# FFT and routed mixture of experts on one core: the gate goes through the second block's gather as three integers, and one of its one-hot matrices gets a scheduling priority

## The chip, the cores and the metric

One core of a Trainium2 chip runs the whole program. Its engines work side by side, each through its own list of instructions in a fixed order: TensorE (PE, matmuls; its weight loads are shown as PEld), VectorE (DVE), ScalarE (ACT), GpSimd (POOL) and SyncE (SP, which here only issues DMAs). The metric is the device time of one execution in microseconds (us), lower is better.

## What is computed

The input x holds 8 batches of 2496 rows of 256 numbers. The real part of its two-dimensional Fourier transform, taken per batch, gives 19968 tokens of 256 numbers. Each token goes to the one expert of eight with the largest logit and is scaled by its softmax probability, the gate:

```python
X = np.fft.fft(np.fft.fft(x, axis=1), axis=2)
x = X.real.astype(np.float32).reshape(B * S, D)
logits = x @ w_gate + modality_bias[modality_id]
e_idx = np.argmax(logits, axis=1)
...
for e in range(E):                      # 8 experts, D = 256, F = 1024
    mask = e_idx == e
    h = np.maximum(x[mask] @ w1[e], 0.0)
    out[mask] = gate_w[mask, None] * (h @ w2[e])
```

## The kernel before

**Two streams of work.** One stream makes the transform and the route, batch by batch: an x tile is loaded (L388), folded on DVE (`fold_add`, the add of L399, 128x1280, and `fold`), its squares are summed on ACT (L402) and PE (L418) to get a scale, matmuls with constant matrices follow (L546; L570 to L590), ACT and DVE split the results into high and low half-precision parts (L524, L525, L221, L222; the tiles rp and rm hold the rows of tokens), and `route` finds the expert and the gate of each token on DVE (L646 to L673, one of them L663, which writes the one-hot choice oh), counts tokens before each other with a matmul by a triangle matrix (L703, L708, which read oh), and scatters the rows to a place per expert in memory (L801, POOL). The other stream prepares the weights of each expert: a load (L955, tile wa), sums of squares on ACT (L965, whose column goes to PE's L418), then a power-of-two scale and the split into a high half on ACT (L995) and a low half on DVE (L996), in tiles w_0, w_1 and w_2.

**Blocks.** Beside these, blocks of tokens run through an expert: L1211 is the first product (48 matmuls in a block of 128 tokens; per group of columns the third matmul reads the low half of the first half of w1, the sixth that of the second half), L1216 and L1217 write relu of it as high and low parts H, L1234 is the second product (24 matmuls, emitted one block later), L1238 and L1241 scale by the gate, L1242 scatters the result to the output. From about 210 us on the program is nearly only such blocks.

**The first three blocks** (128 tokens each, of experts 0, 1 and 2) do not read rows from memory. While the other rows of batch 0 are still on their way there, `onchip` gathers a block's tokens with matmuls: `onehot` (L766) writes a matrix of 117x1536 (12 groups of 128 columns) that has a one where a token's place in the expert's list is the column, PE multiplies rows by it (L782, 48 matmuls in 8 runs of six), ACT casts the result to xT (L785), and PE multiplies the same one-hot by pc (L788, 12 matmuls), a table of six half-precision columns per token: one, the low seven bits and the rest of the token's index, and the gate in three parts. DVE puts index and gate together again (L791 to L797, tile ig). `pieces` writes pc once for all three blocks. A half-precision gate part is the rounding of what the part before has left, times 2048, so L756 to L760 are a chain of five instructions. The one-hot lies in a buffer of its own name Pt, of which there is one, and the fold of x uses the same (L502 to L505).

**What sets the order.** The program is written as generators whose instructions a scheduler sorts, engine by engine, by priority and by its own estimate of times; `hp(n)` is a scope in which the instructions get n more priority. The order is fixed before the run. Two rules in the code tie instructions to `self.made`, the one-hot that was written last: the fold of batch 1 (L399) and the split of the second weight tile (w2 of expert 0) are issued after it.

Of the kernel before, what the change touches and what calls it, by code (L numbers as in the profile page):

```python
# [14 lines left out]
F32 = mybir.dt.float32  # L15
I32 = mybir.dt.int32
I16 = mybir.dt.int16
AF = mybir.ActivationFunctionType
ALU = mybir.AluOpType
# [3 lines left out]
P = 128  # L23
# [6 lines left out]
M3 = 117  # L30
# [219 lines left out]
class Kernel:  # L250
# [494 lines left out]
    def pieces(self, C, dst, gate, part, two):  # L745
        rt, V = self.rt, self.nc.vector
        pc = rt.tile([M3, C, 6], F16, name="pc", bufs=1)
        ix = rt.tile([M3, C], I32, name="pci", bufs=1)
        r = rt.tile([M3, C], F32, name="pcr", bufs=1)
        V.memset(pc[:, :, 0], 1.0)  # L750
        ids = two(self.ids[:, 0])
        V.tensor_scalar(part(ix), ids, 127, None, ALU.bitwise_and)
        V.tensor_copy(pc[:, :, 1], ix)
        V.tensor_scalar(part(ix), ids, 7, None, ALU.logical_shift_right)
        V.tensor_copy(pc[:, :, 2], ix)
        V.tensor_copy(pc[:, :, 3], gate)  # L756
        V.tensor_tensor(r, gate, pc[:, :, 3], ALU.subtract)
        V.tensor_scalar(pc[:, :, 4], r, 2048.0, None, ALU.mult)
        V.scalar_tensor_tensor(r, r, 2048.0, pc[:, :, 4], ALU.mult, ALU.subtract)
        V.tensor_scalar(pc[:, :, 5], r, 2048.0, None, ALU.mult)  # L760
        self.perm = C, dst, pc
        self.inv0 = self.inv[2]

    def onehot(self, C, dst, e):
        oh = self.oh = self.fft.tile([P, NH * P + P], F32, name="Pt", bufs=PQB).bitcast(F16)[:M3, 0:C * P].rearrange("p (c d) -> p c d", c=C)
# [3 lines left out]
    def onchip(self, e):  # L769

        nc, p, rt = self.nc, self.mo, self.rt
        V = nc.vector
        C, dst, pc = self.perm
        cols = [(r, j, s * group.ng + group.g0 + j) for s in range(2) for group in self.groups
                for r in (group.rows2[s],) for j in range(group.gn)]
        if e:
            self.onehot(C, dst, e)
        oh = self.oh
        ps = self.psf.tile([P, 512], F32, name="psf")
        for q in range(4):  # L780
            for k, (r, j, c) in enumerate(cols):
                nc.tensor.matmul(ps[:, q * P:(q + 1) * P], r.bitcast(F16)[:, j, q * P:(q + 1) * P], oh[:, c, :],  # L782
                                 start=k == 0, stop=k == C - 1)
        xT = p.tile([P, 4, P], I16, name="xT128", tag="xT", bufs=3).bitcast(F16)
        nc.scalar.copy(xT, ps.rearrange("p (q c) -> p q c", q=4))  # L785
        ps = self.psf.tile([P, 512], F32, name="psf")
        for k, (r, j, c) in enumerate(cols):
            nc.tensor.matmul(ps[:, 0:6], oh[:, c, :], pc[:, c, :], start=k == 0, stop=k == C - 1)  # L788
        ig = p.tile([P, 1, 2], F32, name="ig128", bufs=8)
        v = rt.tile([P, 6], F32, name="pcv", bufs=2)  # L790
        V.tensor_copy(v, ps[:, 0:6])  # L791
        V.scalar_tensor_tensor(v[:, 1:2], v[:, 2:3], 128.0, v[:, 1:2], ALU.mult, ALU.add)
        V.scalar_tensor_tensor(v[:, 1:2], v[:, 0:1], float(-OOB), v[:, 1:2], ALU.mult, ALU.add)
        V.tensor_scalar(ig.bitcast(I32)[:, 0, 0:1], v[:, 1:2], float(OOB), None, ALU.add)
        V.scalar_tensor_tensor(v[:, 4:5], v[:, 5:6], 1.0 / 2048, v[:, 4:5], ALU.mult, ALU.add)
        V.scalar_tensor_tensor(v[:, 3:4], v[:, 4:5], 1.0 / 2048, v[:, 3:4], ALU.mult, ALU.add)
        V.tensor_scalar(ig[:, 0, 1:2], v[:, 3:4], self.inv0, None, ALU.mult)  # L797
        return xT, ig

# [616 lines left out]
```

## Time and profile before

| | before |
|---|---|
| median of 3 runs | 1059.3 us (1054.3, 1059.3 and 1065.48) |
| the profiled execution, its own time | 1060.53 us |
| its span | 1058.1 us |
| mean granted clock of TensorE | 0.984 of full speed |
| PE busy / DVE busy | 1006.3 us / 560.3 us |

The span is what the trace covers; 2.4 us of the execution's own time lie around it. In a timeline a row is a run of like instructions: its start, its time, the engine, line, operation, output<-inputs, shape and count, and in brackets the idle time just before it with what ended that.

### The profile page before, as it was taken

To read this page: it belongs to the slowest core of one execution; us is meant where nothing else is said; L and a number is where in the kernel's file an instruction comes from. 1 tells how busy PE (TensorE), PEld (TensorE's weight loads), DVE (VectorE), ACT (ScalarE), POOL (GpSimd) and SP (SyncE) were. 2 spreads that over 40 slices of the span, in tenths; PEclk is the share of its full clock that TensorE was granted. 3 is DMA by queue.
4 is the path that set the end of the run, shared out by engine and by line. 5 is a ranking of instruction groups with operands and counts; after the bars stand their busy time and mean duration, and the time that the engine had idled before them with its cause. 6 is when DMAs were issued, how large, how long until landed. Compare 5 with 4: busy or idle time off the path is not lost.

```text
span 1058.1 us, 26309 instructions
## 1 busy us (share of the span) xinstructions
PE 1006.3 (95%) x10019; PEld 902.2 (85%) x10019; DVE 560.3 (53%) x1670; ACT 444.6 (42%) x886; POOL 371.0 (35%) x353
## 2 busy tenths in 40 slices
PE   6788999998999899999999999999999999999996
PEld 5585978986997799999899999988888888899995
DVE  4995969663876673675547553562222222222221
ACT  6674777443534433443334333332323232323331
POOL 0255264263245423443433333343554121221111
PEclk9998999998999999999999999999999999999999
DMA  9678896799499497746966583659888997597790
GB/s 351 248 264 289 200 327 274 195 307 288 132 272 324 138 313 182 210 145 179 285 188 184 163 257 101 192 184 272 214 257 252 301 260 192 149 281 177 205 205 26
DMA packets 151874, 237.66 MB, mean 225 GB/s; under 512 B 115804, under 2 KB 118757, under 8 KB 133565
## 3 DMA queue, kind: packets, MB, share of 16 engines
q1 hardware_dynamic: 132365, 193.75, 63.1%
q0 software_dynamic: 19376, 42.16, 12.4%
q8 instruction: 81, 1.33, 0.5%
q14 instruction: 52, 0.43, 0.1%
HBM read 206.37 MB, written 60.48 MB: 252 GB/s over the span
## 4 chain that ended last, share of the span: by engine, by line
PE 79%; ACT 5%; DVE 4%; issue 4%; DMA 4%; another core or an unknown queue 2%; POOL 1%; SPq 0%; POOLq 0%; ACTq 0%; DVEq 0%
PE pso L1234 35%; PE psm L1211 35%; DMA wa<-w 3%; PE psf L570 2%; PE psf L588 2%; PE psf L544 2%; ACT wj L965 2%; PE psf L575 1%; PE psf L590 1%; DVE H L1217 1%; ACT w L995 1%; ACT H L1216 1%; DMA XM<-x 1%; DVE w L996 1%
## 5 line engine op out<-in xcount | busy, mean ns | idle before, releaser
L1211 PE MATMUL psm<-xT,w 128*128 128x256 f16 (+1 forms) x4512 | 460.1, 258 | 10.2 <-issue 5.7
L1234 PE MATMUL pso<-w,H 128*128 128x256 f16 x3864 | 456.0, 273 | 6.4 <-issue 5.9
L1211 PEld LDWEIGHTS <-w 128*128 128x128 f16 x4512 | 386.9, 98 | 49.0 <-issue 11.4
L1234 PEld LDWEIGHTS <-H 128*128 128x128 f16 x3864 | 375.4, 98 | 53.5 <-issue 10.5
L1217 DVE SCALAR_TENSOR_TENSOR H<-psm,H 128x512 f16<-128x512 f32 x322 | 219.4, 687 | 353.2 <-ACT H L1216 258.9
L1242 POOL DMA_INDIRECT out<-ob,ig x161 | 167.1, 1038 | 455.2 <-ACT ob L1241 414.6
L1216 ACT ACTIVATE H<-psm 128x512 f16<-128x512 f32 x322 | 190.0, 597 | 269.8 <-PE psm L1211 197.5
L1241 ACT ACTIVATE ob<-pso,gs 128x256 f32<-128x256 f32 x161 | 69.0, 471 | 236.8 <-PE pso L1234 217.1
L801 POOL DMA_INDIRECT xd<-rp,dsti x88 | 95.3, 1084 | 103.5 <-DVE H L1217 32.0
L801 POOL DMA_INDIRECT xd<-rm,dsti x88 | 96.9, 1102 | 85.6 <-DVE H L1217 36.1
L525 DVE SCALAR_TENSOR_TENSOR T<-psf,T 120x280 f16<-120x280 f32 (+2 forms) x95 | 43.1, 463 | 71.1 <-ACT T L524 47.6
L524 ACT ACTIVATE T<-psf 120x280 f16<-120x280 f32 (+2 forms) x95 | 38.8, 425 | 17.7 <-PE psm L1211 5.6
L965 ACT ACTIVATE wj<-wa 128x1024 uint8<-128x1024 f32 x32 | 33.9, 1059 | 9.8 <-DMA wa<-w 6.5
L588 PE MATMUL psf<-T,pack 120*117 120x145 f16 x330 | 34.4, 224 | 1.3 <-issue 1.0
L570 PE MATMUL psf<-pack,T 128*120 128x144 f16 (+1 forms) x330 | 32.2, 230 | 0.0
L590 PEld LDWEIGHTS psf<-T,pack 120*117 120x117 f32 x132 | 20.3, 193 | 13.0 <-ACT T L520 5.4
L575 PE MATMUL psf<-m2u,T 128*120 128x280 f32 x88 | 28.4, 451 | 2.7 <-DVE web L407 1.8
L588 PEld LDWEIGHTS <-pack 120*117 120x117 f16 x330 | 28.1, 132 | 2.3 <-issue 1.6
L590 PE MATMUL psf<-T,pack 120*117 120x145 f32 (+1 forms) x132 | 24.1, 306 | 5.8 <-issue 2.3
L996 DVE SCALAR_TENSOR_TENSOR w<-wa,wsc,w 128x1024 f16<-128x1024 f32 (+1 forms) x16 | 28.9, 1806 | 0.9 <-issue 0.9
L399 DVE TENSOR_TENSOR XM<-XM 128x1280 f32<-128x1280 f32 (+2 forms) x18 | 23.7, 1336 | 7.8 <-DMA XM<-x 7.8
L570 PEld LDWEIGHTS <-T 128*120 128x120 f16 x330 | 26.9, 133 | 0.5
(214 smaller groups left out, 664.3 us busy)
## 6 DMA issues: line engine op xcount, KB each, us to landing
w<-w SPq DMA_DIRECT2D x87, 1028.0 KB
w<-w SPq DMA_DIRECT2D x87, 1024.0 KB
XM<-x SPq DMA_DIRECT2D x14, 1280.0 KB
wa<-w SPq DMA_DIRECT2D x16, 1024.0 KB
out<-ob,ig POOLq DMA_INDIRECT x161
XM<-x SPq DMA_DIRECT2D x2, 768.0 KB
xT<-xd SPq DMA_TRANSPOSE x91
xd<-rp,dsti POOLq DMA_INDIRECT x88
```

The costliest lines, as they stand in the source:

```text
L525: self.mark = self.nc.vector.scalar_tensor_tensor(dst[:, 1], ps, scale, dst[:, 0], ALU.mult, ALU.subtract).ins
L570: nc.tensor.matmul(oh, T1[h][:, a, g, :], self.m2h[h][:, w], start=h + k == 0, stop=h * k == 2, skip_group_check=True)
L588: nc.tensor.matmul(ps3[0:M3, cols], self.e3h[:, a, j, :], T2[:, w, cols], start=k == 0, stop=k == 2)
L590: nc.tensor.matmul(ps3[0:M3, cols], self.e3[:, j, :], T2[:, cols], start=True, stop=True)
L801: i = self.nc.gpsimd.indirect_dma_start(out=self.t["xd"], out_offset=bass.IndirectOffsetOnAxis(ap=at, axis=0), in_=row, in_offset=None, bo ...
L965: nc.scalar.activation(jk, x, AF.Square, accum_out=st[:, i:i + 1])
L1211: l1 = nc.tensor.matmul(ps[:, q, :], w1v[:, h, kt, ft], xT[:, xs, :], start=k == 0, stop=k == 5).ins
L1216: nc.scalar.activation(H[:, 0, f0:f0 + NF, :], ps, AF.Relu)
L1217: self.mark = V.scalar_tensor_tensor(H[:, 1, f0:f0 + NF, :], ps, 0.0, H[:, 0, f0:f0 + NF, :], ALU.max, ALU.subtract).ins
L1234: nc.tensor.matmul(po[:, tg, :], H[:, hh, ft, tg * P:(tg + 1) * P], w2v[:, wh, ft, :], start=k == 0, stop=k == 23)
L1241: self.ob = nc.scalar.activation(ob, po[:, tg, :], AF.Identity, scale=gs[:, tg:tg + 1]).ins
L1242: ins = nc.gpsimd.indirect_dma_start(out=t["out"], out_offset=bass.IndirectOffsetOnAxis(ap=ig.bitcast(I32)[:, tg, 0:1], axis=0), in_=ob, i ...
```

## The change

`pieces` multiplies the gate by 2 to the 27 into an integer and takes three fields of nine bits from it, which do not depend on each other, then casts all three to half precision in one instruction; the factor 2 to the -27 goes into a new tile inv0. That is six instructions where there were five. `onchip` puts the parts together with 512 where 1/2048 stood, in the same two instructions. The one-hot of expert 1 (the second block) is emitted with 200 more priority. Line numbers of the changed kernel are 1 or 2 higher behind L760: L766 becomes L767, L782 L784, L996 L998, L1211 L1213, L1217 L1219.

```diff
-        r = rt.tile([M3, C], F32, name="pcr", bufs=1)
+        r = rt.tile([M3, C, 3], I32, name="pcr", bufs=1)
...
-        V.tensor_copy(pc[:, :, 3], gate)
-        V.tensor_tensor(r, gate, pc[:, :, 3], ALU.subtract)
-        V.tensor_scalar(pc[:, :, 4], r, 2048.0, None, ALU.mult)
-        V.scalar_tensor_tensor(r, r, 2048.0, pc[:, :, 4], ALU.mult, ALU.subtract)
-        V.tensor_scalar(pc[:, :, 5], r, 2048.0, None, ALU.mult)
+        V.tensor_scalar(ix, gate, 2.0 ** 27, None, ALU.mult)
+        V.tensor_scalar(r[:, :, 0], ix, 18, None, ALU.logical_shift_right)
+        V.tensor_scalar(r[:, :, 1], ix, 9, 511, ALU.logical_shift_right, ALU.bitwise_and)
+        V.tensor_scalar(r[:, :, 2], ix, 511, None, ALU.bitwise_and)
+        V.tensor_copy(pc[:, :, 3:6], r)
         self.perm = C, dst, pc
-        self.inv0 = self.inv[2]
+        self.inv0 = rt.tile([P, 1], F32, name="inv0", bufs=1)
+        V.tensor_scalar(self.inv0, self.inv[2], 2.0 ** -27, None, ALU.mult)
...
         if e:
-            self.onehot(C, dst, e)
+            with self.hp(200 if e == 1 else 0):
+                self.onehot(C, dst, e)
...
-        V.scalar_tensor_tensor(v[:, 4:5], v[:, 5:6], 1.0 / 2048, v[:, 4:5], ALU.mult, ALU.add)
-        V.scalar_tensor_tensor(v[:, 3:4], v[:, 4:5], 1.0 / 2048, v[:, 3:4], ALU.mult, ALU.add)
+        V.scalar_tensor_tensor(v[:, 4:5], v[:, 3:4], 512.0, v[:, 4:5], ALU.mult, ALU.add)
+        V.scalar_tensor_tensor(v[:, 3:4], v[:, 4:5], 512.0, v[:, 5:6], ALU.mult, ALU.add)
```

The scheduler answers with another order on every engine, up to the point that lies at 209 us in the trace of before; behind it the orders are the same. Three places matter below.

The first is on DVE around the last gate part (L760) and the second one-hot (Pt), while the block of expert 0 is in its first product; before:

```order
L1003 MEMSET w_0_109 128x7
L1217 SCALAR_TENSOR_TENSOR H_566<-psm,H_566 128x512
L760 TENSOR_SCALAR pc<-pcr 117x12
L649 TENSOR_TENSOR L<-L,bias 117x80
L1217 SCALAR_TENSOR_TENSOR H_566<-psm,H_566 128x512
L653 TENSOR_REDUCE mx<-L 117x10
L622 TENSOR_TENSOR bias<-mf,mb 117x176
L791 COPY pcv<-psf 128x6
L766 SCALAR_TENSOR_TENSOR Pt<-dst,pack 117x1536
```

and in the changed kernel:

```order
L760 CAST pc<-pcr 117x12x3
L525 SCALAR_TENSOR_TENSOR rp<-psf,xsc,rp 117x256
L602 COPY Lg<-psf 117x16
L525 SCALAR_TENSOR_TENSOR rp<-psf,xsc,rp 117x256
L602 COPY Lg<-psf 117x16
L234 COPY rp<-tail 117x3x2
L234 COPY rm<-tail 117x3x2
L972 TENSOR_TENSOR wa<-wa 128x1024
L221 COPY rm<-rp 117x3x2x129
L222 TENSOR_SCALAR rm<-rp 117x3x2x127
L767 SCALAR_TENSOR_TENSOR Pt<-dst,pack 117x1536
L793 COPY pcv<-psf 128x6
```

L760 has moved ahead of the evictions L525 and the weight fold L972 (L970 before), and the one-hot L767 ahead of twelve instructions, two of them the low halves of H (L1217, which L1219 is now), that stood before it.

The second is on DVE at the third one-hot and the low halves of expert 1's first weight (w_1_107); before:

```order
L996 SCALAR_TENSOR_TENSOR w_1_107<-wf,wsc,w_1_107 128x1024
L667 TENSOR_TENSOR o_467<-o_465 117x80
L673 TENSOR_TENSOR L<-L,mx 117x80
L996 SCALAR_TENSOR_TENSOR w_1_107<-wa,wsc,w_1_107 128x1024
L969 TENSOR_TENSOR wf<-wa 128x1024
L791 COPY pcv<-psf 128x6
L766 SCALAR_TENSOR_TENSOR Pt<-dst,pack 117x1536
L399 TENSOR_TENSOR XM<-XM 128x1280
L996 SCALAR_TENSOR_TENSOR w_1_110<-wa,wsc,w_1_110 128x2048
```

and in the changed kernel:

```order
L1240 TENSOR_SCALAR gs_871<-ig_559,w_0_109 128x1
L767 SCALAR_TENSOR_TENSOR Pt<-dst,pack 117x1536
L399 TENSOR_TENSOR XM<-XM 128x1280
L656 TENSOR_TENSOR eq<-eq,pack 117x80
L1006 TENSOR_TENSOR w_1_110<-web 128x1
L794 SCALAR_TENSOR_TENSOR pcv<-pcv 128x1
L797 SCALAR_TENSOR_TENSOR pcv<-pcv 128x1
L407 TENSOR_SCALAR web<-psf 128x1
L998 SCALAR_TENSOR_TENSOR w_1_107<-wf,wsc,w_1_107 128x1024
L998 SCALAR_TENSOR_TENSOR w_1_107<-wa,wsc,w_1_107 128x1024
```

Before, both low halves came first; now the third one-hot (L767) and the fold of batch 1 (L399), which is tied to it, stand ahead of them.

The third is on PE ahead of the first block whose rows come from memory (tile w_0_106 is the weight of expert 0); before:

```order
L546 MATMUL psf<-c_75,Qt 128x11x12 x5
L418 LDWEIGHTS ones
L418 MATMUL psf<-wst,ones 128x1
L418 LDWEIGHTS ones
L418 MATMUL psf<-wst,ones 128x1
L1211 LDWEIGHTS w_0_106
L1211 MATMUL psm<-xT_1212,w_0_106 128x128
```

and in the changed kernel:

```order
L546 MATMUL psf<-c_75,Qt 128x11x12 x5
L418 LDWEIGHTS ones
L418 MATMUL psf<-wst,ones 128x1
L418 LDWEIGHTS ones
L418 MATMUL psf<-wst,ones 128x1
L703 LDWEIGHTS tri
L703 MATMUL psf<-oh,tri 128x176
L1213 LDWEIGHTS w_0_106
L1213 MATMUL psm<-xT_1214,w_0_106 128x128
```

L703 of batch 1's route, which before came 72 matmuls later (behind that block's 48 and 24 more of L1234), now stands ahead of the block.

Elsewhere: on ACT the cast of the second block's rows (L787, L785 before) moves ahead of three splits of weights (L995); on SP the load of the second x tile of batch 3 (L388) moves from behind the first transpose of 256 rows (L1195) and three loads of ig (L1198) to ahead of them, and that transpose moves behind two of these loads; and on PE the sum of squares L418 that reads batch 3's nst gets 63 more matmuls ahead of it.

## Rows read from the trace of the kernel before

**Rows 1.** Page: busy time by engine, then the chain that ended last.

```profile
PE 1006.3 (95%) x10019; PEld 902.2 (85%) x10019; DVE 560.3 (53%) x1670; ACT 444.6 (42%) x886; POOL 371.0 (35%) x353
...
PE 79%; ACT 5%; DVE 4%; issue 4%; DMA 4%; another core or an unknown queue 2%; POOL 1%; SPq 0%; POOLq 0%; ACTq 0%; DVEq 0%
```

**Rows 2.** Windows: stretch, length, busy per engine (instructions), granted clock, DMA share, GB/s.

```profile
42.60:81.30 38.70, 31.50 (x432) 29.36 (x431) 37.37 (x128) 27.98 (x47) 20.08 (x13) 0.96 0.73 259
...
54.10:58.10 4.00, 4.00 (x53) 4.00 (x50) 2.67 (x18) 3.97 (x7) 2.15 (x3) 0.57 0.27 81
...
108.60:138.00 29.40, 29.26 (x345) 27.37 (x341) 26.07 (x93) 22.48 (x38) 11.35 (x10) 1.00 0.83 231
...
260.00:1050.00 790.00, 780.41 (x7988) 707.34 (x7986) 369.04 (x1053) 284.50 (x584) 265.03 (x263) 1.00 0.74 210
```

**Rows 3.** Timeline of PE, the three blocks gathered on the chip.

```profile
46.62 2.84 PE L1211 MATMUL psm<-xT,w 128*128 128x128 f16 x48 [1.12 <-ACT xT L785]
50.61 0.46 PE L788 MATMUL psf<-pc,Pt 117*128 117x6 f16 x12 [1.15 <-DVE pc L760]
...
53.47 0.49 PE L782 MATMUL psf<-Pt,rp 117*128 117x128 f16 x6 [2.30 <-DVE Pt L766]
...
54.13 0.84 PE L782 MATMUL psf<-Pt,rp 117*128 117x128 f16 x6
54.76 0.85 PE L782 MATMUL psf<-Pt,rm 117*128 117x128 f16 x6
...
58.08 1.37 PE L546 MATMUL psf<-c,XM 128*128 128x132 f32 x10
60.35 2.84 PE L1211 MATMUL psm<-xT,w 128*128 128x128 f16 x48 [0.91 <-ACT xT L785]
```

**Rows 4.** Timeline of DVE, same stretch.

```profile
46.03 0.17 DVE L758 TENSOR_SCALAR pc<-pcr 117x12 f16<-117x12 f32 x1
...
48.98 0.16 DVE L759 SCALAR_TENSOR_TENSOR pcr<-pcr,pc 117x12 f32<-117x12 f32 x1
...
50.38 0.17 DVE L760 TENSOR_SCALAR pc<-pcr 117x12 f16<-117x12 f32 x1
...
51.67 1.74 DVE L766 SCALAR_TENSOR_TENSOR Pt<-dst,pack 117x1536 f16<-117x1536 f32 x1
...
56.77 1.28 DVE L996 SCALAR_TENSOR_TENSOR w<-wf,wsc,w 128x1024 f16<-128x1024 f32 x1 [1.30 <-ACT w L995]
...
58.24 1.28 DVE L996 SCALAR_TENSOR_TENSOR w<-wa,wsc,w 128x1024 f16<-128x1024 f32 x1
...
62.31 1.48 DVE L399 TENSOR_TENSOR XM<-XM 128x1280 f32<-128x1280 f32 x1
```

**Rows 5.** Timeline of ACT, same stretch.

```profile
55.61 1.13 ACT L995 ACTIVATE w<-wf,wsc 128x1024 f16<-128x1024 f32 x1
...
59.74 0.56 ACT L785 CAST xT<-psf 128x512 f16<-128x512 f32 x1
```

**Rows 6.** Timeline of PE, later points.

```profile
74.45 2.30 PE L1211 MATMUL psm<-xT,w 128*128 128x128 f16 x38 [0.93 <-DVE w L996]
...
79.65 1.11 PE L575 MATMUL psf<-m2u,T 128*120 128x280 f32 x4
...
113.79 0.24 PE L703 MATMUL psf<-oh,tri 117*128 117x176 f16 x1
...
126.74 1.69 PE L1211 MATMUL psm<-xT,w 128*128 128x256 f16 x14
...
166.22 0.16 PE L418 MATMUL psf<-nst,ones 128*128 128x1 bf16 x1 [2.23 <-ACT XM L402]
```

**Rows 7.** Timeline of DVE, the route of batch 1.

```profile
111.58 0.34 DVE L663 TENSOR_TENSOR oh<-pack,ix 117x176 f16<-117x176 f32 x1
```

**Rows 8.** Timeline of SP's queue.

```profile
111.37 1.26 SPq L1195 DMA_TRANSPOSE xT<-xd  x1
...
116.48 0.60 SPq L388 DMA_DIRECT2D XM<-x  x1
```

## Prediction

> **What bounds the kernel now.** I read the page first: PE is busy for 95% of the span, and 79% of the chain that ended last is PE's own work [rows 1]. The windows then say where PE is not busy. From 260 to 1050 us it stands for 9.6 of 790 us and nothing of the change reaches there [rows 2]; what can move lies ahead of the point, at 209 us, from which the two orders agree. In the stretch 42.6 to 81.3 us, where the three gathered blocks run, PE is busy for 31.50 of 38.70 us, so 7.2 us are idle, but DVE is busy for 37.37 of the same 38.70 us [rows 2]. That second number decides: the stretch is DVE's more than PE's. The timeline of PE names the waits one by one: 1.15 us for the last gate part (L760), 2.30 us for the second one-hot (L766), 0.91 us for the cast of the rows of expert 1's block [rows 3]. The first two are what the edit aims at. Behind the second of them the clock falls: from 54.1 to 58.1 us the granted clock is 0.57, near the lower of the two levels, 1.2 against 2.4 GHz [rows 2]; two runs of six L782 matmuls start 0.66 us after the first run (53.47 to 54.13) and one run 0.63 us later (54.13 to 54.76) [rows 3], so 0.33 us a run became 0.63.
>
> **The gate's parts.** Five DVE instructions of 117x12 become six of the same kind, one three times as wide and one of 128x1, at 0.16 to 0.17 us each and with some 0.08 us from start to start where they overlap [rows 4]. Added work is at most 0.3 us of DVE. What matters is the place: L758, L759 and L760 start at 46.03, 48.98 and 50.38 us because each stands where the scheduler left room [rows 4]. Now all parts are done where L758 stood, two small instructions later: 46.03 + 0.15 + 0.17 = 46.35 us instead of 50.55. PE's twelve L788 then run before the first block's L1211 (0.46 us, by the same row of before [rows 3]) and start that block about 0.2 us later; the wait of 1.15 us is gone.
>
> **The second one-hot.** In the first piece of the order it stands right behind an L222, so it starts where L759 stood, 48.98 plus 0.2, about 49.2 us, and ends at 49.2 + 1.74 = 50.95 us; before it ran from 51.67 to 53.41 [rows 4]. The gather L782 follows at about 51.0 instead of 53.47 us [rows 3]: 2.5 us earlier. With no wait ahead of it I take the clock as full, so eight runs take 8 x 0.33 = 2.7 us, L788 0.35 and L546 1.3 us, to about 55.35 us. ACT cannot cast before its squares of a weight end, which is where L995 stands, at 55.61 us; the cast now follows right there and takes 0.56 us [rows 5]. So the first product of expert 1's block begins at about 56.25 us instead of 60.35, which is 4.1 us earlier.
>
> **Where the stall goes.** The price is in the second piece of the order. The twelve instructions that the one-hot passed, two evictions of 0.6 us among them, come later, then the third one-hot (1.74 us as the second, which cannot start before the second gather has freed the one buffer, at about 54.1 us) and the fold L399 (1.48 us), and only then the two low halves of expert 1's w1. They were done at 56.77 + 1.28 = 58.05 and 58.24 + 1.28 = 59.52 us [rows 4]. Walking DVE's new order with the durations of the trace, the third one-hot starts at about 54.7, the fold ends at about 57.8, and the low halves end at about 59.4 and 60.6 us. The block's third matmul reads the first half, its sixth the second. So PE does two matmuls at 56.3 and waits some 3 us, then again some 1 us, and the rest of the block runs from 60.6, just when it ran before (60.35 plus five matmuls). Of 4.1 us saved, about 0.1 is left. The same can be had without the walk: the instructions that DVE must do before PE's L575 at 79.65 us [rows 6] are the same in both orders, and DVE has 38.70 - 37.37 = 1.33 us of idle time to give back [rows 2]; the block of expert 2 too waits for DVE (0.93 us for a low half of weights [rows 6]). The gain at 79.65 us lies between 0 and 1.3 us; I take 0, since the walk ends at 79.5 to 79.9.
>
> **The route of batch 1.** In the third piece PE meets L703 at 108.5 us, ahead of a block that before started there. L703 reads oh, which DVE writes with L663 from 111.58 to 111.92 us [rows 7], in a stretch where DVE is busy for 26.07 of 29.40 us [rows 2], and nothing of the change moves DVE's rows ahead of L663 by more than a place. Before, 72 matmuls covered this wait, and L703 ran at 113.79 [rows 6]. Now PE stands from 108.6 to about 111.9: **+3.3 us**. The block behind it fills PE later; nothing else was missing it. Bounds: 0, if DVE comes there 3.3 us earlier, and 3.3.
>
> **What is given back.** At 166.22 us PE waits 2.23 us for the squares of batch 3 (L402), ahead of L418 [rows 6]. With 63 more matmuls in front, some 7 us of work at 0.11 us each (2.84 us for 48 of 128 columns and twice that for 256), that wait is covered: **-2.2 us**. Bounds: 0 and -2.23.
>
> **The sum.** 0 + 3.3 - 2.2 = +1.1 us on 1060.53, 1061.6 us for a profiled execution. That execution is 1.2 us above the median of the three runs shown, 1059.3, so I expect 1060.0 to 1060.4 and say 1060.0 us. The likeliest case by itself lies between -1.3 + 0 - 2.2 = -3.5 and 0 + 3.3 + 0 = +3.3 us: 1056 to 1063.
>
> **Rivals.** (1) *Faster: the waits removed stay removed.* If DVE comes to the low halves in time, because small instructions overlap more than I count, PE keeps the 2.30 us, the five groups of L782 at half clock (5 x 0.30 = 1.5 us), and the 2.2 us at 166: 1059.3 - 6.0 = 1053. For it speaks that these waits are the largest of the stretch; against it the 1.33 us of DVE's idle time. Chance 0.2. (2) *Slower: a transpose is late.* On SP's queue the first transpose of 256 rows was issued at 111.37 us, ahead of the load of XM at 116.48 [rows 8]. Now it stands behind this load, which has a buffer to wait for, and behind two loads of ig. Its block started at 126.74 us [rows 6], 15.4 us after the issue. If the issue slips to 118 or later, the block could start at about 133.5, while PE, 3.3 us late, is there at 130.0: another 3.5 us, and up to 7 if PE's lateness does not arise; 1060 + 3.5 to 7 gives 1064 to 1067. It decides from the point where that block's first matmul comes after 131 us with an idle time that ends on a DMA. Against it: PE has other work in the order beside that block (L546, L578). Chance 0.2. (3) *The clock.* Where PE now waits 3 us ahead of a block's third matmul, the granted clock may fall as it did behind the 2.30 us of before, and 46 matmuls go at 0.105 instead of 0.055 us: +2.3 us, 1062. Chance 0.1. (4) *The edit does nothing there*, because L760 and the one-hot are held by their inputs (the gate, the places) and not by their order: 1059. The inputs of L759 were there at 46.2 us and it ran at 48.98 [rows 4], which speaks against it. It lies within the likeliest range; chance 0.05.
>
> On (3) a rule can be set beside the rows. The Trainium skill, "TensorE: Matmul & The Clock Gate", Part 1 on the clock gate, says that the throttled level is the default, and that activity releases it. By it, PE's waits near 50 us are what brought the half clock in L782, and shifting them elsewhere shifts that stretch instead of removing it; the rows of before agree as far as they go, since the granted 0.57 follows the waits of 1.15 and 2.30 us. By that rule the sum would be 1062; I keep full speed in the sum because the waits of before that were as long as 2.23 us, at 166 us, left no row that I read at the lower level.
>
> **How the numbers follow.** Likeliest, no change that can be seen: 0.45; faster 0.2; late transpose 0.2; clock 0.1; no effect 0.05. One percent, 10.6 us, is about what a measurement of this kernel tells from no change. None of the cases reaches it alone: the faster one would need 4 us more, the slower one 3. So within 1% has 0.85, faster 0.08, slower 0.07. The range from 1052 to 1067 holds all the cases but their far ends.
>
> **What would show it.** Right: L788 of expert 0's block ahead of its L1213; the second one-hot at 49 to 50 us; PE idle some 3 us inside the first product of expert 1's block with a low half of w1 (L998) as the releaser; L575 of batch 1 within 1 us of 79.65; a wait of about 3 us ahead of L703 that ends on DVE's oh; no wait at L418 near 166 us. Wrong: L575 first at 76 us or earlier, or L703 without a wait (then it is faster), or the first 256-token block behind a DMA (then slower).

## The result and the profile after

The changed kernel needs 1066.53 us (median of 22 runs, 1058.87 to 1070.65), the kernel before 1057.69 us in the same comparison (22 runs, 1052.11 to 1065.48): a ratio of 1.008 with a 95% interval of 1.0061 to 1.0098. The change costs 0.8%, 8.8 us by the medians. It was said to cost 1.1 us, and "within 1%" was the likeliest case. The time lies inside the range, just under its upper end, and beyond the likeliest case's own range of 1056 to 1063: the direction of the sum was right, and its size was not.

The profiled execution of after took 1069.0 us (span 1067.1, mean granted clock 0.979; before 1060.53, 1058.1 and 0.984). The page's busy line and its chain that ended last, which answer to [rows 1]:

```profile
PE 1009.3 (95%) x10019; PEld 904.8 (85%) x10019; DVE 561.4 (53%) x1671; ACT 444.3 (42%) x886; POOL 371.2 (35%) x353
...
PE 77%; DVE 7%; issue 5%; DMA 3%; ACT 2%; another core or an unknown queue 2%; SPq 2%; POOL 1%; POOLq 0%; ACTq 0%; DVEq 0%
```

PE's work is what it was (3.0 us more busy time, with the half clock shown below), but DVE's share of the chain went from 4% to 7%. Windows of after, laid where the same work stands as in [rows 2] (stretch, length, busy by engine with counts, granted clock, DMA share, GB/s):

```profile
45.10:84.00 38.90, 33.02 (x429) 31.59 (x427) 34.94 (x100) 26.72 (x44) 18.75 (x12) 0.87 0.67 232
...
63.10:69.20 6.10, 6.02 (x63) 6.02 (x63) 6.10 (x10) 2.03 (x6) 0.00 (x0) 0.51 0.51 168
112.00:147.00 35.00, 30.76 (x344) 28.70 (x345) 31.67 (x109) 22.93 (x40) 14.38 (x11) 0.95 0.87 243
117.70:121.70 4.00, 4.00 (x50) 4.00 (x50) 3.86 (x15) 1.01 (x3) 0.00 (x0) 0.67 0.01 4
269.00:1059.00 790.00, 780.79 (x7990) 707.01 (x7988) 369.12 (x1054) 284.10 (x584) 264.89 (x263) 1.00 0.74 211
```

The last row says that nothing moved late: 780.79 of 790 us, 780.41 before. In the stretch of the three gathered blocks DVE, which the prediction took for the bound with 1.33 us to spare, now stands idle for 3.96 of 38.90 us, and PE runs at half clock (0.51, close to 1.2 of 2.4 GHz) from 63.1 to 69.2 us. (The first gather of after, from 45.2 to 48.5 us, also runs at half clock, 0.50, behind a wait of 1.99 us that ends on ACT's L520; in before it does not.) The timeline of PE in after, of that stretch (start, length, instruction, the idle time before it and who ended it):

```profile
50.33 2.84 PE L1213 MATMUL psm<-xT,w 128*128 128x128 f16 x48 [0.39 <-ACT xT L787]
...
53.46 0.49 PE L784 MATMUL psf<-Pt,rp 117*128 117x128 f16 x6 [0.21 <-DVE Pt L767]
...
56.45 1.37 PE L546 MATMUL psf<-c,XM 128*128 128x132 f32 x10
59.23 0.52 PE L418 MATMUL psf<-wst,ones 128*128 128x1 bf16 x4 [1.41 <-ACT wj L967]
60.28 0.40 PE L1213 MATMUL psm<-xT,w 128*128 128x128 f16 x4 [0.53 <-ACT w L997]
63.18 0.80 PE L784 MATMUL psf<-Pt,rp 117*128 117x128 f16 x6 [2.50 <-DVE web L407]
63.77 0.85 PE L784 MATMUL psf<-Pt,rm 117*128 117x128 f16 x6
```

The two waits that the edit aims at are gone: 0.21 us for the second one-hot in place of 2.30, and none for a gate part [rows 3]. In their place PE stands 2.50 us ahead of the third gather, whose groups then start 0.6 us apart and not 0.33. DVE in after, where that wait is made:

```profile
51.67 1.74 DVE L767 SCALAR_TENSOR_TENSOR Pt<-dst,pack 117x1536 f16<-117x1536 f32 x1
...
59.35 0.16 DVE L793 COPY pcv<-psf 128x6 f32<-128x6 f32 x1 [2.28 <-remote]
...
59.55 1.75 DVE L767 SCALAR_TENSOR_TENSOR Pt<-dst,pack 117x1536 f16<-117x1536 f32 x1
61.22 1.48 DVE L399 TENSOR_TENSOR XM<-XM 128x1280 f32<-128x1280 f32 x1
...
62.98 0.15 DVE L407 TENSOR_SCALAR web<-psf 128x1 f32<-128x1 f32 x1
63.05 1.27 DVE L998 SCALAR_TENSOR_TENSOR w<-wf,wsc,w 128x1024 f16<-128x1024 f32 x1
```

The third gather has its one-hot at 61.3 us, but by the profile it waits for L407, which reads psum, the memory that the gather writes to, and L407 stands behind the one-hot and the fold. Ahead of both DVE stood still for 2.28 us. The later points of PE in after, which answer to [rows 6]:

```profile
113.46 0.19 PE L418 MATMUL psf<-wst,ones 128*128 128x1 bf16 x2
117.66 0.31 PE L703 MATMUL psf<-oh,tri 117*128 117x176 f16 x1 [4.01 <-DVE oh L663]
117.76 4.07 PE L1213 MATMUL psm<-xT,w 128*128 128x128 f16 x48
...
137.30 1.47 PE L1213 MATMUL psm<-xT,w 128*128 128x256 f16 x12
...
157.56 0.19 PE L418 MATMUL psf<-wst,ones 128*128 128x1 bf16 x2 [2.66 <-DVE web L407]
```

L703 makes PE wait 4.01 us, and the 48 matmuls behind it take 4.07 us where they take 2.84 at full speed [rows 3]. The wait of 2.23 us for the squares of batch 3 (L402) is found nowhere in after, but one of 2.66 us on DVE (L407) stands at 157.56 us.

### The profile page after: what moved, and what is told of

It reads as the page before. It is cut to its first block, busy times and chain, and to the rows that moved or that the text cites. A ratio compares the mean times of both kernels' runs of the same rounds, so it can differ in the third digit from the quotient of the medians.

```text
span 1067.1 us, 26308 instructions
## 1 busy us (share of the span) xinstructions
PE 1009.3 (95%) x10019; PEld 904.8 (85%) x10019; DVE 561.4 (53%) x1671; ACT 444.3 (42%) x886; POOL 371.2 (35%) x353
## 3 DMA queue, kind: packets, MB, share of 16 engines
q8 instruction: 81, 1.33, 0.5%
## 4 chain that ended last, share of the span: by engine, by line
PE 77%; DVE 7%; issue 5%; DMA 3%; ACT 2%; another core or an unknown queue 2%; SPq 2%; POOL 1%; POOLq 0%; ACTq 0%; DVEq 0%
PE pso L1236 34%; PE psm L1213 34%; PE psf L570 2%; PE psf L588 2%; PE psf L575 2%; PE psf L544 1%; PE psf L590 1%; DVE w L998 1%; DVE H L1219 1%; DMA wa<-w 1%; DMA XM<-x 1%; DMA xd<-rm,dsti 1%; POOL out L1244 1%; ACT wj L967 1%
## 5 line engine op out<-in xcount | busy, mean ns | idle before, releaser
L1213 PE MATMUL psm<-xT,w 128*128 128x256 f16 (+1 forms) x4512 | 462.0, 258 | 8.8 <-issue 5.1
L1213 PEld LDWEIGHTS <-w 128*128 128x128 f16 x4512 | 387.9, 98 | 51.9 <-issue 14.4
L1219 DVE SCALAR_TENSOR_TENSOR H<-psm,H 128x512 f16<-128x512 f32 x322 | 218.9, 687 | 351.6 <-ACT H L1218 276.2
L1244 POOL DMA_INDIRECT out<-ob,ig x161 | 163.6, 1016 | 452.9 <-ACT ob L1243 384.2
L803 POOL DMA_INDIRECT xd<-rp,dsti x88 | 98.6, 1120 | 118.4 <-DVE H L1219 43.2
L525 DVE SCALAR_TENSOR_TENSOR T<-psf,T 120x280 f16<-120x280 f32 (+2 forms) x95 | 43.2, 464 | 70.1 <-ACT T L524 40.4
L590 PEld LDWEIGHTS psf<-T,pack 120*117 120x117 f32 x132 | 19.9, 193 | 14.1 <-ACT T L520 6.4
L590 PE MATMUL psf<-T,pack 120*117 120x145 f32 (+1 forms) x132 | 23.8, 304 | 8.4 <-issue 4.2
L575 PE MATMUL psf<-m2u,T 128*120 128x280 f32 x88 | 28.8, 456 | 1.8 <-ACT T L520 0.8
L998 DVE SCALAR_TENSOR_TENSOR w<-wa,wsc,w 128x1024 f16<-128x1024 f32 (+1 forms) x16 | 29.0, 1810 | 2.2 <-ACT w L997 1.1
L399 DVE TENSOR_TENSOR XM<-XM 128x1280 f32<-128x1280 f32 (+2 forms) x18 | 23.7, 1337 | 7.8 <-DMA XM<-x 7.8
```

The costliest lines, as they stand in the source:

```text
L575: self.pe23 = nc.tensor.matmul(ps[0:120, 0:280], T1[h][:, g, :], self.m2u[h], start=h == 0, stop=h == 1).ins
L590: nc.tensor.matmul(ps3[0:M3, cols], self.e3[:, j, :], T2[:, cols], start=True, stop=True)
L803: i = self.nc.gpsimd.indirect_dma_start(out=self.t["xd"], out_offset=bass.IndirectOffsetOnAxis(ap=at, axis=0), in_=row, in_offset=None, bo ...
L1213: l1 = nc.tensor.matmul(ps[:, q, :], w1v[:, h, kt, ft], xT[:, xs, :], start=k == 0, stop=k == 5).ins
L1219: self.mark = V.scalar_tensor_tensor(H[:, 1, f0:f0 + NF, :], ps, 0.0, H[:, 0, f0:f0 + NF, :], ALU.max, ALU.subtract).ins
L1244: ins = nc.gpsimd.indirect_dma_start(out=t["out"], out_offset=bass.IndirectOffsetOnAxis(ap=ig.bitcast(I32)[:, tg, 0:1], axis=0), in_=ob, i ...
```

## The experiments

They were run in five sessions, each with the kernel before beside them. The sessions are of two kinds that must be told apart, because the kernel before itself differs between them: in some sessions it needs 1056 to 1059 us, as in the comparison above, in others 1037 to 1038 us. PE's waits behind 215 us show the difference. For the kernel before above (who waited on what: us in all, times, the longest):

```profile
PE psm L1211 <- issue: 5.3, 9, 1.0
PE pso L1234 <- issue: 4.7, 8, 1.0
PE psf L588 <- issue: 1.0, 2, 0.5
```

In a session of the other kind no such row exists; for the integer gates alone the whole answer is

```profile
engine line waited for: us in total, times, longest us
PE pso L1235 <- ACT ob L1242: 0.6, 1, 0.6
```

I call the first kind sessions with issue waits and the second quiet ones. Each ratio is against the kernel before in the same session.

**Which half of the change moves the order?** The integer gates without the priority, in a quiet session:

```diff
-            with self.hp(200 if e == 1 else 0):
-                self.onehot(C, dst, e)
+            self.onehot(C, dst, e)
```

> The integer gates of the change, with the second one-hot at its old priority. The orders say that the gates alone bring nearly all of the new order (third one-hot and fold ahead of the low halves of expert 1's w1, L703 ahead of the block of expert 0 from memory). Theory A (the order that follows from the gates costs the time): as slow as the change, 1.005 to 1.010 of before. Rival B (the priority costs it): within 0.2% of before.

and the priority alone, put into the kernel before:

```diff
-            self.onehot(C, dst, e)
+            with self.hp(200 if e == 1 else 0):
+                self.onehot(C, dst, e)
```

> The old chain of gate parts, with 200 more priority for the second one-hot. On DVE four rows move by one place, on the other engines none. Theory A: within 0.2% of before, second one-hot at about 51.6 us as in rows 4. Rival B (the priority costs the time): 1.005 or more.

Measured: 1035.48 us, 0.9996 (0.9984 to 1.0008), and 1037.27 us, 1.0005 (0.999 to 1.0021). The orders settle the first question: the gates alone give practically the change's whole new order (third one-hot and fold ahead of the low halves, L703 ahead of the block from memory), while the priority alone moves four of DVE's rows by one place. But neither moved the time, so the loss had to be sought where it arises.

**Does undoing the two moved places undo the loss?** The change with its third one-hot held behind the low halves of expert 1's w1, and then with L703 of batch 1 held behind the first matmuls of the block from memory as well, in the same quiet session:

```diff
-            with self.hp(200 if e == 1 else 0):
+            with self.hp(200 if e == 1 else 0), ExitStack() as st:
+                if e == 2:
+                    st.enter_context(self.tc.issue_after(self.low[2]))
```

> The change, with the third one-hot tied behind the first low half of expert 1's w1 (order on PE then: whole first product of expert 1's block ahead of the third gather, as before); L703 stays ahead of the block from memory. Theory A: of the change's 8.8 us about 5 come back (the waits of 2.50 us at the third gather and the half clock behind it), 1.003 to 1.005 of before, L575 of batch 1 about 5 us earlier against its own start than in the change, and the wait of about 4 us at L703 stays. Rival (DVE gives back nothing, it is only shifted): as slow as the change, 1.007 to 1.010.

```diff
+        if b == 1:
+            st.enter_context(tc.issue_after(self.l1s[3]))
         m = nc.tensor.matmul(ps[:, 0:8 * C], self.tri[:, 0, :], ...
```

> The change, with the third one-hot behind the first low half of expert 1's w1 and L703 of batch 1 behind the first product of the block from memory. PE then has the order of before in this part, but with L788 of expert 0's block early and the second one-hot early. Theory A: the waits of 1.15 and 2.30 us are saved and nothing is paid for them: 0.994 to 0.999 of before. Rival C (DVE is the bound of the stretch, the saving is given back at its low halves; or the loss lies ahead of 46 us): 0.999 to 1.006.

Measured: 1038.83 us, 1.0026 (1.0015 to 1.0037), and 1038.27 us, 1.0014 (0.9999 to 1.0028). There was no loss here to undo, and the first tie even costs a little.

**The change again, and L703 alone put back**, in a session with issue waits. The second kernel is the change with the last diff only:

> The change itself once more, beside the kernel before, perhaps on another chip than in the first comparison. If the loss belongs to the order (theory A): 1.006 to 1.010 wherever it runs. If it belongs to the chip of the first comparison, whose traces hold waits of PE with no releaser (15.3 us of 'issue' after 40 us in before, none on the chip of the runs with gates alone and priority alone; theory D): 0.998 to 1.002 on a chip without such waits.

> The kernel before, for a trace on the same chip as the change. Theory D: no waits for 'issue' on PE behind 215 us, and the block from memory waits some 5 us for its transposed rows at 108 us, as with the priority alone; theory A: waits as in the first trace of before.

> The change with L703 of batch 1 tied behind the first product of the block from memory. Theory A: the wait of some 4 us at L703 is gone, the block starts about 3.5 us earlier, 0.996 to 0.998 of the change. Rival E (the block then waits for the DMA of its rows instead): the wait at the block's first matmul takes its place, 0.999 to 1.002 of the change.

Measured: the change 1068.1 us, 1.0108 (1.0077 to 1.0139); before once more 1053.57 us (a single execution); L703 behind 1069.27 us, 1.0117 (1.0084 to 1.0149). So the loss belongs to this kind of session. In the change again L703 and the block behind it, timeline of PE:

```profile
117.36 0.30 PE L703 MATMUL psf<-oh,tri 117*128 117x176 f16 x1 [4.01 <-DVE oh L663]
117.45 4.91 PE L1213 MATMUL psm<-xT,w 128*128 128x128 f16 x48
```

and the window behind it, with the clock at 0.54:

```profile
117.40:122.20 4.80, 4.80 (x49) 4.80 (x49) 4.66 (x23) 0.96 (x3) 0.00 (x0) 0.54 0.18 28
```

The same block in the kernel before, measured beside it, starts without a wait and at full speed:

```profile
111.30 2.84 PE L1211 MATMUL psm<-xT,w 128*128 128x128 f16 x48
113.98 2.78 PE L1234 MATMUL pso<-w,H 128*128 128x256 f16 x24
116.60 0.24 PE L703 MATMUL psf<-oh,tri 117*128 117x176 f16 x1
```

With L703 put behind, its wait is gone and the block starts 4.6 us earlier than in the change again, at full speed, yet nothing is won. The timeline of PE of that kernel has new waits farther on:

```profile
112.81 2.84 PE L1215 MATMUL psm<-xT,w 128*128 128x128 f16 x48
...
121.43 1.50 PE L1215 MATMUL psm<-xT,w 128*128 128x128 f16 x24 [1.46 <-DVE H L1221]
123.64 1.69 PE L1239 MATMUL pso<-w,H 128*128 128x256 f16 x14 [0.71 <-ACT ob L1246]
126.64 1.26 PE L1239 MATMUL pso<-w,H 128*128 128x256 f16 x10 [1.30 <-DVE H L1221]
146.08 0.84 PE L578 MATMUL psf<-m2p,T 128*120 128x144 f32 x2 [6.24 <-issue]
149.01 1.25 PE L1215 MATMUL psm<-xT,w 128*128 128x256 f16 x5 [1.02 <-DVE H L1221]
```

The tie does not move L703 alone: the scheduler plans everything behind it anew, and sets splits of weights ahead of an eviction of H, for which PE then waits 1.30 us. The longest wait, 6.24 us, is of another sort: DVE itself stands still for 5.04 us ahead of it, in a stop that ends on nothing in the trace. So the time of this run does not price L703 by itself; what its timeline says of that place stands in the table below.

**The gates alone and both ties, in a session with issue waits**, beside the change a third time:

> The change again, for a comparison with the gates alone and with both ties on one chip. Where PE has waits for 'issue' behind 215 us: 1.007 to 1.012. Where it has none (as on the chip of the gates alone, 0.9996): theory D says 0.998 to 1.002, theory F (the priority adds its part to the gates) 1.004 or more.

> The integer gates alone. Theory D (the chip decides, the priority moves next to nothing): within 0.2% of the change on the same chip. Theory F (the priority costs the difference): within 0.2% of before.

> The change with the third one-hot behind a low half of expert 1's w1 and L703 of batch 1 behind the block's first product, so that PE's order up to 130 us is nearly that of before. Theory A (the order of the third one-hot and of L703 costs the time): 0.997 to 1.003 of before wherever it runs, so about 1% under the change where the change is slow. Rival (the time goes behind 130 us, or to chance in the order): as slow as the change.

Measured: the change 1066.76 us, 1.0089 (1.0052 to 1.0125); the gates alone 1067.51 us, 1.0101 (1.0059 to 1.0143); both ties 1063.79 us, 1.0056 (1.0026 to 1.0085). The priority adds nothing: the gates alone cost what the change costs. The ties take back a third or so by the medians, but the intervals overlap, and both ties together do not bring back the time of the kernel before, as had been expected if the two moved places were all of the loss.

The gates alone were profiled in both kinds, so one program shows what a session adds. DVE in the session with issue waits:

```profile
54.28 0.22 DVE L655 TENSOR_TENSOR eq<-L,mx 117x80 f32<-117x80 f32 x1
56.37 0.16 DVE L792 COPY pcv<-psf 128x6 f32<-128x6 f32 x1 [1.86 <-PE psf L546]
56.45 1.75 DVE L767 SCALAR_TENSOR_TENSOR Pt<-dst,pack 117x1536 f16<-117x1536 f32 x1
```

and in the quiet one:

```profile
54.38 0.23 DVE L655 TENSOR_TENSOR eq<-L,mx 117x80 f32<-117x80 f32 x1
54.52 0.15 DVE L792 COPY pcv<-psf 128x6 f32<-128x6 f32 x1
54.60 1.74 DVE L767 SCALAR_TENSOR_TENSOR Pt<-dst,pack 117x1536 f16<-117x1536 f32 x1
```

L792 reads the second gather's last small products, which end at 54.2 and 54.3 us. In the quiet session it follows at once, before the L546 that the other profile names as its releaser is done. In the session with issue waits DVE stands still for 1.86 us. PE's wait ahead of the third gather follows, in the session with issue waits and then in the quiet one:

```profile
60.25 0.80 PE L783 MATMUL psf<-Pt,rp 117*128 117x128 f16 x6 [2.20 <-DVE web L407]
...
58.40 0.80 PE L783 MATMUL psf<-Pt,rp 117*128 117x128 f16 x6 [0.38 <-DVE web L407]
```

All four profiles of the whole change have this stop of DVE, of 2.25 to 2.29 us, and so have both kernels with L703 behind, of 2.27 and 2.31 us; the two profiles of the kernel before in such sessions show no idle time of DVE longer than 1.30 us in that stretch.

The other half is L703. The gates alone in the quiet session, PE:

```profile
103.93 0.30 PE L703 MATMUL psf<-oh,tri 117*128 117x176 f16 x1 [3.86 <-DVE oh L663]
104.31 5.10 PE L1212 MATMUL psm<-xT,w 128*128 128x128 f16 x48
```

and the order of before (the priority alone) in the same session:

```profile
103.00 0.19 PE L418 MATMUL psf<-wst,ones 128*128 128x1 bf16 x2
108.67 4.44 PE L1212 MATMUL psm<-xT,w 128*128 128x128 f16 x48 [5.48 <-DMA xT<-xd]
```

L703 waits as long in the quiet session, but there it costs nothing. In the order of before PE comes to the block at 103 us, before its rows have landed, and waits 5.48 us for the transpose. SP's queue issued that transpose, with the gates alone and then in the order of before, at:

```profile
100.75 1.32 SPq L1196 DMA_TRANSPOSE xT<-xd  x1
...
105.07 1.32 SPq L1196 DMA_TRANSPOSE xT<-xd  x1
```

The block that waits for the transpose starts 3.60 us after its issue, and with the gates alone the block starts 3.56 us after it. So the rows came about when L703 was done, and its wait hid behind theirs; the slow matmuls that follow the wait come in both orders (5.10 and 4.44 us). In the session with issue waits the kernel before comes to the block at 111.30 us and finds the rows there, so the wait of L703 has nothing to hide behind.

**Last, the one-hot's tie alone and the change a fourth time**, each in a session of its own:

> The change with its third one-hot (and the fold tied to it) behind the low halves of expert 1's w1, without the tie of L703, on a chip that may have issue waits or not. Where PE has none behind 215 us (before near 1037 us), it should again be within 0.3% of before. Where it has them (before near 1056 us), the theory that the 8 us are made by two things, the half clock behind the 2.5 us wait near 60 us and the uncovered wait of 4 us at L703, says that this tie alone takes away at most the first, so PE still stands some 4 us at L703 and the ratio is near 1.007; the rival that the third one-hot's place alone makes the loss says 1.00 to 1.003.

> The change itself once more. Theory: it costs 8 to 11 us (ratio 1.008 to 1.011) where PE and DVE show waits marked issue and before needs near 1056 us, and nothing measurable (0.998 to 1.002) where PE shows none behind 215 us and before needs near 1037 us, since PE then comes to the first block of rows from memory before its transposes have landed and the wait of L703 hides behind them. Rival: the integer gates alone cost nothing there, but the change as a whole does (1.005 or more on any chip).

Measured: the tie 1038.38 us beside 1038.24 (quiet), 1.0002 (0.9984 to 1.002); the change 1066.78 us beside 1059.41 (issue waits), 1.0074 (1.0047 to 1.0101). Both sessions report the same chip number, so the number does not tell the two kinds apart. The change as a whole was not measured in a quiet session; that it costs nothing there rests on the gates alone, whose order is practically its own. The priority by itself was not measured in a session with issue waits.

None of these kernels beats the kernel before by more than the noise.

## Why the prediction was right, and where its sum failed

The table gives how much later PE reaches the same matmul than in the profile of before, in us, worked out from the timelines of PE and good to about 0.1; the first column says which matmul, and its time in before. After, fourth, again and third are profiles of the change, gates is the integer gates alone, and the last two columns are the kernels that take L703's wait away. All are from sessions with issue waits.

| matmul, time in before | before again | after | fourth | again | third | gates | L703 behind | both ties |
|---|---|---|---|---|---|---|---|---|
| first product, expert 0, 46.68 | 0.6 | 3.7 | 2.8 | 0.5 | 1.2 | 1.3 | 1.2 | 1.0 |
| second product, expert 2, 78.98 | 0.5 | 2.7 | 1.9 | 0.6 | 0.2 | 0.3 | 0.2 | 3.9 |
| last L575 ahead of the block, 102.97 | 2.8 | 5.0 | 4.2 | 4.7 | 2.2 | 3.9 | 4.3 | 4.9 |
| second block from memory, 115.99 | 2.8 | 10.4 | 9.6 | 10.9 | 7.8 | 9.9 | 5.9 | 5.8 |
| 215.06 | -0.1 | 9.9 | 7.8 | 11.0 | 7.0 | 9.8 | 9.0 | 7.7 |
| 1040.26 | -6.4 | 9.0 | 6.5 | 8.3 | 5.9 | 8.2 | 7.7 | 4.3 |

Single executions wander by several us (the first column of offsets); what all five of the new order share counts. From 102.97 to 115.99 each loses 5.4 to 6.2 us and the kernel before nothing. That is the main term. With L703's wait taken away the same stretch costs 1.6 and 0.9 us, so most of the term is this wait and what follows it. But both of these kernels lose 1.9 to 3.1 us farther on to 215 us, where the five lose nothing, and both ties lose 2.8 us in the gathered blocks as well: that the wait of L703 makes the loss of the whole kernel is read from its place in the timelines, and no run shows it by giving the time back.

- **The stretch of the gathered blocks: 0, from 0 to 1.3 us of gain. Right, by a way that was half wrong.** From 46.68 to 78.98 us the new order changes by -1.0, -0.9, +0.2, -1.0 and -1.0 us. The waits went as said: the second gather starts at 50.91 us in the change's third profile (51.0 said), the cast of its rows at 55.79 (55.61 said), and PE ends L546 about 4 us earlier, for 4.1 said (in the change again the second gather still waits 1.29 us for its one-hot). And the gain was given back behind the third one-hot, as said. But the releaser was not a low half of w1: it was L407, which frees the psum tile that the third gather writes. With the ties the wait sits on the low half as the walk had it (2.95 and 0.65 us in the session with issue waits, 0.92 and 0.96 in the quiet one with the one-hot's tie alone). And the argument "DVE is the bound, with 1.33 us to give back" failed: DVE's stop of 2.3 us, which no row of before could show, eats what the new order would have won. In the quiet session, without it, the third one-hot of the gates alone starts at 54.60 us (54.7 said), and they gain 3.1 us on the order of before from 46.7 to 79 us.
- **The wait of L703: +3.3, measured 4.0.** Place, releaser (oh, L663) and cause stood as forecast. Said was an upper bound of 3.3; it is 3.86 to 4.01. In after L663 starts 5.7 us later than in before (117.26 for 111.58), and PE is only 5.0 us later.
- **What is missing: the half clock behind that wait.** The 48 matmuls take 4.07 to 4.91 us in place of 2.84, so +1.2 to 2.1 us. This is the step that failed. The sum took full speed behind every new wait, on the argument that the 2.23 us at 166 us had left no row at the lower level. That reading of before was wrong: behind that wait the granted clock is 0.58 from 166.25 to 169.50 us (rows below the list). Behind 4.0 us of idle the granted clock was 0.54 in the change again. The clock was weighed as rival 3 with 2.3 us, but at the first product of expert 1's block and not here; the half clock came in both stretches, as 0.51 at 63 us in after, though there in the third gather for the most part, and as 0.54 at 117 us in the change again. "TensorE: Matmul & The Clock Gate" of the Trainium skill, Part 1, has the throttled level as the default, released by activity; the rows agree, with half-clock matmuls behind the waits of 2.50 and 4.0 us. By that rule, which the prediction set aside, the new wait ahead of L703 would have been costed with such matmuls behind it.
- **The give-back at 166 us: -2.2, measured about 0.** The wait for the squares is gone as said, but from 115.99 to 215.06 us the five profiles change by -0.5, -1.8, +0.1, -0.8 and -0.1 us, because waits of 2.66 us (after) and 1.96 us (third) on DVE's L407, or of 2 to 3 us marked issue in all, stand at 155 to 161 us instead. It is the second step that failed: the smallest gain it allowed was 0, and the full 2.2 was taken.

Four matmuls of L590 in the profile of before, at the half clock behind the wait of 2.23 us and then at full speed:

```profile
166.90 1.14 PE L590 MATMUL psf<-T,pack 120*117 120x145 f32 x4
...
171.16 0.64 PE L590 MATMUL psf<-T,pack 120*117 120x145 f32 x4
```

Put together, by means over the five and over the two of before: -0.7 for the gathered blocks, +5.7 for L703 and its half clock, and +0.8 from there to 215 us make 5.8 us where 1.1 was said. Of the 9.1 us at 215 us, 1.6 stand already at 46.68 us and 1.7 arise from 79 to 103 us. These two differ between executions of the same program by as much (0.5 to 3.7 at the first point), and I can't tie them to the change. Behind 215 us the orders are the same; that before again gains 6.3 us there goes with its shorter issue waits (5.8 us of them on PE, 11.0 in before).

That the time stayed inside the range is partly luck: the range reached up to 1067 us for the late transpose, which did not come, and the loss came from a step that the sum had put at nothing and another that it had taken for a gain.

**The rivals.** (1) did not come: the 4 us were given back by 79 us. (2) did not: the transpose of 256 rows slipped to 123.64 us, as said to behind the load of XM, but its block starts at 137.30 us without a wait, because PE is later too. (3) came, with the wait that it named in another place. (4) is refuted, since the one-hot ran where the order put it.

## What to carry to other kernels

A wait that moves on PE must be costed with the clock behind it: some 4 us of idle went with a loss of 5.4 to 6.2 us here. An instruction that waits is free only while something else holds the engine at that place, and which of the two ends last can differ between sessions: the same L703 cost nothing where PE came too early for its rows. And a lone tie or priority in a planned order is not a lone move; look at the order behind it before reading its time as the price of one wait.

## What was not expected of the hardware

The same program took 1037 us in some sessions and 1056 to 1059 in others. In the slower ones PE shows waits that end on nothing in the trace (11.0 us of them behind 215 us in before, none there in the quiet ones), and DVE stops at one and the same place of the new orders in all seven of their profiles from such sessions. The kernel before has such stops elsewhere (3.43 and 3.54 us at 89 us in its two profiles), and the quiet sessions are not free of them: each of the five profiles taken there has one DVE stop of 4.5 to 6.9 us, marked issue, that ends between 132 and 142 us. What makes them is not settled: the chip's number was the same once for both kinds, and the transfers of instructions that the page counts stand in both in the same numbers (81 and 52 packets).
